# Talking-heads attention into routed experts: 512-column products in the experts' first layer, and another order at the loop's end

## Chip, cores and metric

One core of a Trainium2 chip runs the whole program. The metric is the device time of one execution in microseconds (us), and the median of several runs is compared. Its engines are TensorE (PE in the profile, with PEld for its weight loads), VectorE (DVE), ScalarE (ACT), GpSimd (POOL) and SyncE (SP). SP issues the plain DMAs, and POOL issues the indirect ones (gathers and scatters by index).

## What is computed

Attention first, with 4 batches, 12 heads, 448 positions and 64 values a head. Heads are mixed before and after the softmax. The result is then laid out as 1792 tokens of 768 values, and each token goes through one of 8 experts:

```python
scores = np.einsum('bhij,hg->bgij', scale * q @ k.T, w_pre)
attn = softmax(scores)
attn = np.einsum('bhij,hg->bgij', attn, w_post)
x = (attn @ v).transpose(0, 2, 1, 3).reshape(1792, 768)

logits = normed(x) @ normed(expert_emb).T / tau
expert_idx = np.argmax(logits, axis=1)
gate_w = softmax(logits)[token, expert_idx]
for e in range(8):
    mask = expert_idx == e
    h = np.maximum(x[mask] @ w1[e], 0.0)              # 768 -> 1024
    out[mask] = gate_w[mask, None] * (h @ w2[e])      # 1024 -> 768
```

## The kernel before, in words

**Attention.** The tokens are cut into 16 tiles of 120 or 90 positions, and a tile into 5 or 6 steps, 92 steps in all. A step of the loop multiplies q by k (L262), mixes heads (L297), takes the softmax (L305, L314), mixes again and transposes (L340, L345) and evicts the result `a` to SBUF (L358 on ACT, L360 on DVE). One tile later the product with v follows (`emit_av`, L376). Its sum lies in one PSUM bank (`ps_a`, one buffer), which `emit_xT_evict` (L388, on ACT) copies out. `emit_xlog` (L394) transposes it back and makes the routing logits, and `emit_x` (L406) and `store_x` (L414) write tokens to `x_tok` in DRAM.

**The order** of everything is written out by hand: each engine runs its instructions in the order in which the program lists them, and waits inside its queue for what it needs. Side work of the loop is held in generators that are advanced twice a step: `route_early` (positions of the first 10 tiles within their experts; its last product is `p_i`, L538), `gate_value` (gates; eight small stores into `g_tok`, L494), `first_x` (gather of the first expert's first rows, L604, and of their gates, L610, on POOL), `mid`. A bank for them is taken only at steps that `pes_at` leaves free.

**Weights.** All expert products are float32r products of split numbers: a weight is split into `wh` and the rest `wl`, x into `xh` and `xl`, h into `hh` and `hl`. `w_split` does one slice of 128 weight rows: `wh` on ACT (L590), `wl` on DVE (L591). It also issues the DMA (L575, on SP) of slices up to four ahead, into four `raw_w` buffers, each of which comes free when its `wl` is done. An expert has 14 slices: 8 of w2 (768 columns, 384 KB) and 6 of the next expert's w1 (1024 columns, 512 KB).

**Experts.** Expert 0 and the last, overflow tile (128 rows whose expert is chosen at run time) go through `ffn_tok`. It keeps rows of x on the weight side and multiplies 512 columns of w1 at a time (L644); then `relu`, a transpose `tr` (L653, evicted as `hh` on ACT, L656, and `hl` on DVE, L657) and products with w2 (L663). Calls to `w_split` stand between its steps. Experts 1 to 7 have 256 rows each: `emit_g1` keeps w1 on the weight side. For each of 8 blocks of 128 columns and each of 6 slices it makes three products of 256 columns (wh by xh, wh by xl, wl by xh, L1049) into half a bank. A pair of blocks fills a bank, which is evicted by `hh` (ACT, L1051) and `hl` (DVE, L1052). After each pair `during_g1` transposes part of the next expert's x (`fill`: L624, L629, L630), does two splits and one step of `route_late` (positions of overflow rows; pairs of L1138, L1139 on DVE). `emit_g2` multiplies by w2 (L1067) for two halves `j` of the rows and two halves `n0` of the columns, scales by the gate (L1069) and scatters (L697).

Of the kernel before, what the change touches and what calls it, by code (L numbers as in the profile page):

```python
# [32 lines left out]
MAXO = 12  # L33
# [14 lines left out]
def talking_heads_moe(  # L48
# [81 lines left out]
    with tc.manual_schedule():  # L130
# [409 lines left out]
        def route_early(bank, wait):  # L540
# [9 lines left out]
            pairs = yield from place(re, p, 0, NE)  # L550
            yield from wait()
# [62 lines left out]
        def emit_xT(pool, xgs):  # L614

            b = 1 if pool is xa_p else 2
            xh = pool.tile([128, KD, 128 * b], FR, tag="xh", name="xh", bufs=b)[:, :, :128 * len(xgs)]
            xl = pool.tile([128, KD, 128 * b], FR, tag="xl", name="xl", bufs=b)[:, :, :128 * len(xgs)]
# [15 lines left out]
            return (xh, xl), [lambda j=j, k0=k0: step(j, k0) for j in range(len(xgs)) for k0 in (0, 3)]  # L634
# [148 lines left out]
        for t in range(NTL - 1):  # L783
# [5 lines left out]
            for k, p in ((0, b0 + 2), (1, b0 + ln - 1)):  # L789
                if k and t == NTL - 2:  # L790
                    continue
                acts.setdefault(p, []).append(lambda t=t, k=k: emit_xT_evict(t, k))
# [127 lines left out]
        emit_xT_evict(LT - 1, 1)  # L920
# [8 lines left out]
        w_split(V, 2)  # L929
        w_split(V, 2)  # L930
        for a in range(3):
            emit_av(LT, a)
        late_lo = []
        w_split(V, 2, late_lo.append)
        w_split(V, 2, late_lo.append)
        run(gens[-1][0])
        for f in late_lo:
            f()
        emit_xlog(LT - 1, 1)
        emit_xT_evict(LT, 0)  # L940
        emit_lgc(LT - 1, 1)
        emit_x(LT - 1, 1)
        store_x(LT - 1)
# [55 lines left out]
        for f in late_lo:  # L999
            f()  # L1000
# [3 lines left out]
        xT, fill = emit_xT(mp, xg[0])  # L1004
        slots(iv, 0, 2 * E)
# [30 lines left out]

        def emit_g1(xT, w, after):
            xh, xl = xT
# [3 lines left out]
            for f0 in range(0, KF, 2):  # L1042
                p = ps_h.tile([128, 512], F32, tag="p", name="p_h").rearrange("p (f n) -> p f n", n=n)
                for f in range(2):
                    c = slice((f0 + f) * 128, (f0 + f + 1) * 128)
                    for k in range(KD):
                        wh_, wl_ = w[k]
                        for i, (lt, rt_) in enumerate(((wh_, xh), (wh_, xl), (wl_, xh))):
                            T.matmul(p[:, f], lt[:, c], rt_[:, k], start=(k == 0 and i == 0), stop=(k == KD - 1 and i == 2))  # L1049
                o = (slice(None), slice(f0, f0 + 2))  # L1050
                A.activation(out=hh[o], in_=p, func=ACTF.Relu)  # L1051
# [21 lines left out]
        def route_late():  # L1073
# [55 lines left out]
            for t in range(NTL + 2):  # L1129
                if t > 1:  # L1130
                    T.matmul(xb[:, 16:16 + MAXO], *hot[t - 2], start=(t == 2), stop=(t == NTL + 1))
# [131 lines left out]
```

## Time and profile before

| | |
|---|---|
| three runs | 716.62, 713.16 and 710.42 us (median 713.16) |
| profiled execution | 712.93 us, its span 711.1 us |
| mean granted TensorE clock | 0.987 of full speed |
| PE busy | 676.7 us, 95% of the span |
| DVE busy | 463.2 us, 65% |
| ACT busy | 393.6 us, 55% |
| POOL busy | 119.1 us, 17% |
| DMA | 134.61 MB, 189 GB/s on average |

The span runs from the first to the last instruction; the execution's own time has 1.83 us more around it. Busy shares are averages over the attention loop (to about 378 us), the end of the loop and expert 0 (378 to 430 us), experts 1 to 7 (430 to 677 us), the overflow tile (677 to 700 us) and a tail with the last scatter.

### The profile page before, as it was taken

How to read it: one execution, taken by the hardware profiler on the slowest of the kernel's cores; microseconds unless marked ns; L12 is line 12 of the kernel's file. 1: busy time of each engine (PE TensorE's matmuls, PEld its weight loads, DVE VectorE, ACT ScalarE, POOL GpSimd, SP SyncE). 2: the span in 40 equal slices, each digit the busy share in tenths (PEclk: the TensorE clock that was granted, in tenths of full speed). 3: DMA queues.
4: the chain of work that ended last, by engine and by line, in shares of the span. 5: the costliest groups of instructions: out<-in, count | busy, mean ns of one | idle time of the engine just before them, and what ended most of it. 6: DMA issues, size and time to landing. Idle time of an engine off the chain costs nothing. (4 is left out here: it accounts for less than half of the span.)

```text
span 711.1 us, 25384 instructions
## 1 busy us (share of the span) xinstructions
PE 676.7 (95%) x10796; PEld 559.6 (79%) x10796; DVE 463.2 (65%) x1076; ACT 393.6 (55%) x775; POOL 119.1 (17%) x179
## 2 busy tenths in 40 slices
PE   9799999999999999989998899999999999999983
PEld 4366776776777777767777789999999999999973
DVE  6477666666667666886676765868665656474651
ACT  2466676667767676756676453635262636353540
POOL 7021010110111011101201213430203030100000
PEclk9899999999999999999999999999999999999997
DMA  7687567655667556643614755867676767575750
GB/s 224 187 247 214 150 197 212 194 171 160 194 201 212 177 162 193 202 134 116 214 47 128 261 164 154 292 206 224 205 227 213 233 216 233 182 235 170 249 155 15
DMA packets 60361, 134.61 MB, mean 189 GB/s; under 512 B 7067, under 2 KB 38411, under 8 KB 60246
## 3 DMA queue, kind: packets, MB, share of 16 engines
q1 hardware_dynamic: 56126, 119.56, 54.7%
q0 software_dynamic: 3520, 12.44, 5.2%
q8 instruction: 86, 1.41, 0.8%
q10 hardware_dynamic: 600, 0.97, 0.4%
q14 instruction: 29, 0.24, 0.1%
HBM read 83.21 MB, written 12.20 MB: 134 GB/s over the span
## 5 line engine op out<-in xcount | busy, mean ns | idle before, releaser
L305 DVE TENSOR_REDUCE mn<-p_p 128x1 f32<-128x448 f32 (+1 forms) x182 | 105.6, 619 | 91.2 <-PE p_p L297 90.4
L590 ACT ACTIVATE wh<-raw_w 128x768 fp32r<-128x768 f32 (+2 forms) x132 | 114.9, 904 | 45.5 <-DMA raw_w<-w 42.6
L591 DVE TENSOR_TENSOR wl<-raw_w,wh 128x768 fp32r<-128x768 f32 (+2 forms) x132 | 131.0, 1026 | 9.4 <-ACT wh L590 9.1
L270 ACT ACTIVATE s<-p_q 128x896 f32<-128x896 f32 (+1 forms) x89 | 80.8, 909 | 91.3 <-PE p_q L262 81.4
L314 ACT ACTIVATE e<-p_p,mn 128x448 f32<-128x448 f32 (+1 forms) x182 | 113.5, 628 | 31.9 <-DVE mn L305 28.0
L340 PEld LDWEIGHTS p_m<-wr,e 64*64 64x64 f32 x4320 | 84.0, 135 | 44.8 <-issue 41.7
L360 DVE COPY a<-p_m 128x420 f32<-128x420 f32 (+1 forms) x182 | 95.0, 562 | 2.8 <-PE p_m L345 2.6
L1049 PE MATMUL p_h<-xh,wh 128*128 128x256 f32 x336 | 96.8, 288 | 0.0
L262 PE MATMUL p_q<-k,q 64*64 64x448 f32 x768 | 96.4, 569 | 0.3 <-ACT s L270 0.3
L376 PE MATMUL p_av<-a,v 128*64 128x120 f32 (+3 forms) x1920 | 92.0, 248 | 3.1 <-issue 2.0
L1049 PE MATMUL p_h<-xh,wl 128*128 128x256 f32 x336 | 94.9, 283 | 0.0
L1049 PE MATMUL p_h<-xl,wh 128*128 128x256 f32 x336 | 94.7, 282 | 0.0
L297 PE MATMUL p_p<-g,wpre_sb 64*64 64x448 f32 (+1 forms) x712 | 89.4, 544 | 5.1 <-DMA g<-s 4.7
L376 PEld LDWEIGHTS p_av<-a,v 128*64 128x64 f32 x1920 | 83.3, 137 | 9.3 <-issue 3.8
L340 PE MATMUL p_m<-wr,e 64*64 64x60 f32 x4320 | 85.1, 219 | 3.7 <-issue 1.7
L325 POOL TENSOR_TENSOR wr<-wpost_sb,r 128x120 f32<-128x120 f32 (+1 forms) x92 | 35.5, 386 | 314.1 <-DVE r L324 218.2
L1067 PE MATMUL p_o<-wh,hh 128*128 128x384 f32 x224 | 75.8, 338 | 0.0
L1067 PE MATMUL p_o<-wh,hl 128*128 128x384 f32 x224 | 75.0, 335 | 0.0
L1067 PE MATMUL p_o<-wl,hh 128*128 128x384 f32 x224 | 75.0, 335 | 0.0
L1051 ACT ACTIVATE hh<-p_h 128x512 fp32r<-128x512 f32 x28 | 16.7, 598 | 100.6 <-PE p_h L1049 63.6
L297 PEld LDWEIGHTS p_p<-g,wpre_sb 64*64 64x64 f32 (+1 forms) x712 | 30.2, 134 | 43.2 <-issue 31.4
L1049 PEld LDWEIGHTS p_h<-xl,wh 128*128 128x128 f32 x336 | 63.6, 189 | 0.0
(209 smaller groups left out, 951.1 us busy)
## 6 DMA issues: line engine op xcount, KB each, us to landing
g<-s SPq DMA_DIRECT2D x144, 210.0 KB
raw_w<-w SPq DMA_DIRECT2D x54, 512.0 KB
raw_w<-w SPq DMA_DIRECT2D x72, 384.0 KB
v<-vP SPq DMA_DIRECT2D x24, 320.0 KB
g<-s SPq DMA_DIRECT2D x42, 157.5 KB
k<-kT SPq DMA_DIRECT2D x24, 224.0 KB
q<-qT SPq DMA_DIRECT2D x26, 192.0 KB
x_tok<-xs SPq DMA_DIRECT2D x22, 180.0 KB
```

The lines of the kernel that those rows point to most:

```text
L262: T.matmul(p[r][64 * w:64 * w + 64, :S], q_sb[t][64 * r:64 * r + 64, a, w, :], k_sb[t // 4, a][64 * r:64 * r + 64], start=True, stop=True)
L270: A.activation(out=o, in_=i, func=ACTF.Copy)
L297: T.matmul(p[w][64 * x:64 * x + 64, :S], wpre_sb[64 * w:64 * w + 64 - 4 * w], g[64 * w:64 * w + 64 - 4 * w, m + x if nx == 2 else m], star ...
L305: V.tensor_reduce(out=mn[q, c:c + 1], in_=p[u][q, :S], op=ALU.max, axis=AX.X, negate=True)
L314: A.activation(out=e[q, c], in_=p[u][q, :S], func=ACTF.Exp, bias=mn[q, c:c + 1], accum_out=sums[q, c:c + 1])
L340: T.matmul(pm[x][q[c], u * 240 + jt * 60:u * 240 + jt * 60 + 60], e[q[x], u, jt * 128 + 64 * c:jt * 128 + 64 * c + 64], wr[q[x], u], start ...
L360: V.tensor_copy(out=o, in_=i)
L376: T.matmul(p[64 * r:64 * r + 64, u], v_sb[t // 4, a][:, jt, r * D:(r + 1) * D], at[:, jt * 12 + c::48][:, :2] if jt < 3 else at[:, 36 + c] ...
L590: A.activation(out=h[:, c], in_=r[:, c], func=ACTF.Copy)
L591: lo = lambda: eng.tensor_tensor(out=l[:, c], in0=r[:, c], in1=h[:, c].bitcast(F32), op=ALU.subtract)
L1049: T.matmul(p[:, f], lt[:, c], rt_[:, k], start=(k == 0 and i == 0), stop=(k == KD - 1 and i == 2))
L1067: T.matmul(p[:, :384], lt[:, k, c], rt_[:, m], start=(k == 0 and i == 0), stop=(k == KF - 1 and i == 2))
```

## The change

- `route_early` pauses twice more between `place` and its last product.
- `emit_xT` puts xh and xl of a slice side by side in one tile `xx`.
- At the loop's end the second half of tile 14 is evicted (L388) inside the last step, ahead of that step's weight split on ACT. Its `emit_xlog` goes ahead of the products of tile 15 with v, and its `emit_x`, logits and store directly behind the first three of these. Two half splits move back by some places.
- In expert 0 one step of `ffn_tok` (its first `tr` among others) goes ahead of two `wl` operations and two small operations on DVE.
- In `emit_g1` each slice is two products: wh by xh and xl together, 512 columns wide, and wl by xh, 256 columns, added onto the half that holds wh by xl. Each block of 128 columns has a bank of its own, in turn two of `ps_h` and the one of `ps_a`. To evict it, ACT copies the second half out (`hx`) and DVE adds the first (`hs`); `hh` and `hl` are then made from the pair of sums in SBUF.
- In `emit_g2` the first half of the rows runs six slices for both column halves and then the last two for both.
- Splits: seven during `emit_g1`, seven during `emit_g2`. `route_late` is advanced in `emit_g1` from expert 2 on only, and its products follow their DVE operations by four tiles where it was two.
- In the overflow tile three splits that stood ahead of the first `tr` go behind it.

```diff
             pairs = yield from place(re, p, 0, NE)
+            yield
+            yield
             yield from wait()
             p = bank("p_i")
...
             for k, p in ((0, b0 + 2), (1, b0 + ln - 1)):
+                acts.setdefault(p, []).append(lambda t=t, k=k: emit_xT_evict(t, k))
                 if k and t == NTL - 2:
                     continue
-                acts.setdefault(p, []).append(lambda t=t, k=k: emit_xT_evict(t, k))
...
         evict()
-        emit_xT_evict(LT - 1, 1)
...
         closing.append(True)
-        w_split(V, 2)
+        emit_xlog(LT - 1, 1)
         w_split(V, 2)
         for a in range(3):
             emit_av(LT, a)
+        emit_x(LT - 1, 1)
+        emit_lgc(LT - 1, 1)
+        store_x(LT - 1)
         late_lo = []
         w_split(V, 2, late_lo.append)
         w_split(V, 2, late_lo.append)
         run(gens[-1][0])
+        emit_xT_evict(LT, 0)
         for f in late_lo:
             f()
-        emit_xlog(LT - 1, 1)
-        emit_xT_evict(LT, 0)
-        emit_lgc(LT - 1, 1)
-        emit_x(LT - 1, 1)
-        store_x(LT - 1)
+        w_split(V, 2)
         w_split(V, 2)
         emit_sq(LT - 1, rt)
...
-        for f in late_lo:
-            f()
         w1p[1] = weight(w1, 1, KD, F, "a")
...
         xT, fill = emit_xT(mp, xg[0])
+        steps_of(st_a, 1)
+        for f in late_lo:
+            f()
         slots(iv, 0, 2 * E)
...
             for f0 in range(0, KF, 2):
-                p = ps_h.tile([128, 512], F32, tag="p", name="p_h").rearrange("p (f n) -> p f n", n=n)
+                hs = mp.tile([128, 2, n], F32, tag="hs", name="hs", bufs=1)
                 for f in range(2):
+                    p = ps_a.tile([128, 512], F32, tag="a", name="p_h") if turn[0] % 3 == 2 else (
+                        ps_h.tile([128, 512], F32, tag="p", name="p_h"))
+                    turn[0] += 1
                     c = slice((f0 + f) * 128, (f0 + f + 1) * 128)
                     for k in range(KD):
-                        wh_, wl_ = w[k]
-                        for i, (lt, rt_) in enumerate(((wh_, xh), (wh_, xl), (wl_, xh))):
-                            T.matmul(p[:, f], lt[:, c], rt_[:, k], start=(k == 0 and i == 0), stop=(k == KD - 1 and i == 2))
+                        wide = (p, w[k][0][:, c], xx[:, k].rearrange("p a n -> p (a n)"))
+                        small = (p[:, n:], w[k][1][:, c], xh[:, k])
+                        for i, m in enumerate((wide, small) if k < KD - 1 else (small, wide)):
+                            T.matmul(*m, start=(k == 0 and i == 0), stop=(k == KD - 1 and i == 1))
+                    hx = mp.tile([128, n], F32, tag="hx", name="hx", bufs=2)
+                    A.activation(out=hx, in_=p[:, n:], func=ACTF.Copy)
+                    V.tensor_tensor(out=hs[:, f], in0=p[:, :n], in1=hx, op=ALU.add)
                 o = (slice(None), slice(f0, f0 + 2))
-                A.activation(out=hh[o], in_=p, func=ACTF.Relu)
-                V.scalar_tensor_tensor(out=hl[o], in0=p, scalar=0.0, in1=hh[o].bitcast(F32), op0=ALU.max, op1=ALU.subtract)
+                A.activation(out=hh[o], in_=hs, func=ACTF.Relu)
+                V.scalar_tensor_tensor(out=hl[o], in0=hs, scalar=0.0, in1=hh[o].bitcast(F32), op0=ALU.max, op1=ALU.subtract)
                 after(f0 // 2)
...
-                for n0 in range(2):
-                    p = ps_m.tile([128, 512], F32, tag="m", name="p_o")
+                p = {}
+                for n0, ks in ((0, range(6)), (1, range(6)), (0, range(6, KF)), (1, range(6, KF))) if j == 0 else (
+                        (0, range(KF)), (1, range(KF))):
...
+                    if ks[-1] == KF - 1:
+                        V.tensor_scalar(out=o[:, m], in0=p[n0], scalar1=gj[:, 0:1], scalar2=None, op0=ALU.mult)
+                        after(2 * j + n0)
+                    else:
+                        w_split(V)
...
             def during_g1(q):
...
                 w_split(V)
-                w_split(V)
-                next(late, None)
+                if q < 3:
+                    w_split(V)
+                if e > 1:
+                    next(late, None)
...
             def during_g2(q):
                 if q < 3:
                     w_split(V)
+                if q < 2:
                     w_split(V)
                 next(late, None)
...
         for i, _ in enumerate(ffn_tok(xT, w1p[E], w2p[E], gg[E][0], idx_s[:, 2 * E:2 * E + 1])):
-            if i != KD - 1:
-                w_split(V)
-            if i == KD:
+            if i < KD - 1 or i in (2 * KD - 2, 2 * KD, 2 * KD + 1):
                 w_split(V)
```

## Rows read from the trace of the kernel before

**Rows 1.** Busy time by stretch: us, each engine (instructions), PEclk, DMA share, GB/s.

```profile
398.00:410.00 12.00, 10.08 (x60) 9.43 (x59) 7.49 (x12) 4.52 (x8) 4.09 (x3) 1.00 0.94 343
430.00:686.00 256.00, 256.00 (x1816) 253.62 (x1816) 163.92 (x254) 117.04 (x159) 51.55 (x43) 1.00 0.69 221
686.00:692.00 6.00, 3.27 (x11) 2.58 (x10) 3.47 (x4) 2.78 (x5) 0.00 (x0) 0.77 0.05 22
```

**Rows 2.** Waits of PE, 290 to 400 us: waiter, releaser, total, times, longest.

```profile
PE p_i L538 <- DVE ohs L532: 0.9, 1, 0.9
```

**Rows 3.** Timeline of PE, first layer of expert 1: start, duration; twelve products apart.

```profile
439.87 0.28 PE L1049 MATMUL p_h<-xh,wh 128*128 128x256 f32 x1
...
441.31 0.28 PE L1049 MATMUL p_h<-xh,wh 128*128 128x256 f32 x1
```

**Rows 4.** Timeline of PE, first layer of expert 0: again twelve products apart.

```profile
389.37 0.40 PE L644 MATMUL p_h<-wl,xh 128*128 128x512 f32 x1
...
392.11 0.39 PE L644 MATMUL p_h<-wl,xh 128*128 128x512 f32 x1
```

**Rows 5.** Timeline of DVE, first layer of expert 3.

```profile
511.58 0.69 DVE L1052 SCALAR_TENSOR_TENSOR hl<-p_h,hh 128x512 fp32r<-128x512 f32 x1 [1.04 <-ACT hh L1051]
512.19 0.55 DVE L630 TENSOR_TENSOR xl<-p_t,xh 128x384 fp32r<-128x384 f32 x1
512.69 1.83 DVE L591 TENSOR_TENSOR wl<-raw_w,wh 128x768 fp32r<-128x768 f32 x2
516.33 0.69 DVE L1052 SCALAR_TENSOR_TENSOR hl<-p_h,hh 128x512 fp32r<-128x512 f32 x1 [1.81 <-ACT hh L1051]
```

**Rows 6.** Timeline of ACT, the same stretch.

```profile
510.95 0.60 ACT L1051 ACTIVATE hh<-p_h 128x512 fp32r<-128x512 f32 x1 [2.33 <-PE p_h L1049]
511.44 0.49 ACT L629 ACTIVATE xh<-p_t 128x384 fp32r<-128x384 f32 x1
```

**Rows 7.** Groups of ACT, 425 to 700 us: count, busy us, mean ns, idle before.

```profile
L590 ACT ACTIVATE wh<-raw_w 128x768 fp32r<-128x768 f32 x64 | 51.0, 846 | 7.2 <-DMA raw_w<-w 6.1 <-SPq L1186 1.0
L590 ACT ACTIVATE wh<-raw_w 128x1024 fp32r<-128x1024 f32 x45 | 47.8, 1062 | 34.2 <-DMA raw_w<-w 32.5 <-DVE ohp L1138 0.8 <-DVE wl L591 0.4
```

**Rows 8.** Groups of DVE, 425 to 700 us: one operation of a late-routing pair.

```profile
L1139 DVE TENSOR_SCALAR ohs<-io,mo,tv 128x12 f16<-128x12 f32 x16 | 4.6, 290 | 0.0
```

**Rows 9.** Timeline of PE at the end of the loop.

```profile
378.00 0.30 PE L345 MATMUL p_m<-wr,e 64*64 64x60 f32 x4
379.46 2.30 PE L376 MATMUL p_av<-a,v 128*64 128x90 f32 x60 [1.16 <-ACT xT L388]
...
382.15 0.94 PE L394 MATMUL p_x<-ien,xT 128*120 128x136 f32 x6
...
386.51 0.93 PE L394 MATMUL p_x<-ien,xT_l 128*90 128x136 f32 x6 [0.30 <-ACT xs L406]
```

**Rows 10.** Timeline of ACT and of DVE at the last step.

```profile
376.37 0.61 ACT L590 ACTIVATE wh<-raw_w 128x512 fp32r<-128x512 f32 x1
...
376.97 1.29 DVE L591 TENSOR_TENSOR wl<-raw_w,wh 128x512 fp32r<-128x512 f32 x2
```

**Rows 11.** Timelines of PE and ACT in expert 0, first tile.

```profile
399.72 0.45 PE L663 MATMUL p_o<-wh,hl 128*128 128x384 f32 x1 [1.48 <-DVE hl L657]
...
402.57 0.85 ACT L590 ACTIVATE wh<-raw_w 128x768 fp32r<-128x768 f32 x1 [1.81 <-DMA raw_w<-w]
```

**Rows 12.** Timelines of SP and POOL: the gates' stores, and their first gather.

```profile
335.43 3.33 SPq L494 DMA_DIRECT2D g_tok<-gt__6303  x8
...
353.52 1.01 POOL L610 DMA_INDIRECT gg<-g_tok,idx_a  x1 [0.30 <-issue]
```

**Rows 13.** Timelines of DVE and PE in the overflow tile.

```profile
686.16 2.91 DVE L591 TENSOR_TENSOR wl<-raw_w,wh 128x768 fp32r<-128x768 f32 x3 [1.20 <-ACT wh L590]
688.62 0.44 PE L663 MATMUL p_o<-wh,hh 128*128 128x384 f32 x1 [2.06 <-ACT hh L656]
689.73 0.69 PE L663 MATMUL p_o<-wh,hl 128*128 128x384 f32 x1 [0.67 <-DVE hl L657]
```

More of the change, by code (lines that the diff above doesn't have):

```diff
@@ L616, in emit_xT @@
             b = 1 if pool is xa_p else 2
-            xh = pool.tile([128, KD, 128 * b], FR, tag="xh", name="xh", bufs=b)[:, :, :128 * len(xgs)]
-            xl = pool.tile([128, KD, 128 * b], FR, tag="xl", name="xl", bufs=b)[:, :, :128 * len(xgs)]
+            xx = pool.tile([128, KD, 2, 128 * b], FR, tag="xx", name="xx", bufs=b)
+            xh, xl = (xx[:, :, i, :128 * len(xgs)] for i in range(2))
             def step(j, k0):
@@ L633, in step @@
                 split()
-            return (xh, xl), [lambda j=j, k0=k0: step(j, k0) for j in range(len(xgs)) for k0 in (0, 3)]
+            return (xh, xl, xx), [lambda j=j, k0=k0: step(j, k0) for j in range(len(xgs)) for k0 in (0, 3)]
         def ffn_tok(xT, w1, w2, gg, ix, held=None):
@@ L1035, in talking_heads_moe @@
         rows_of(2, x=False)
+        turn = [0]
         def emit_g1(xT, w, after):
-            xh, xl = xT
+            xh, _, xx = xT
             n = xh.shape[2]
@@ L1060, in emit_g2 @@
                 c = slice(128 * j, 128 * j + 128)
[L1061 to L1062 removed]
+                p = {}
+                for n0, ks in ((0, range(6)), (1, range(6)), (0, range(6, KF)), (1, range(6, KF))) if j == 0 else (
+                        (0, range(KF)), (1, range(KF))):
                     m = slice(384 * n0, 384 * n0 + 384)
[L1064 removed]
+                    if ks[0] == 0:
+                        p[n0] = ps_m.tile([128, 512], F32, tag="m", name="p_o")[:, :384]
+                    for k in ks:
                         wh_, wl_ = w[k]
                         for i, (lt, rt_) in enumerate(((hh, wh_), (hl, wh_), (hh, wl_))):
[L1067 removed]
+                            T.matmul(p[n0], lt[:, k, c], rt_[:, m], start=(k == 0 and i == 0),
                                      stop=(k == KF - 1 and i == 2))
[L1069 to L1070 removed]
+                    if ks[-1] == KF - 1:
[3 more added lines that the diff above has]
+                        w_split(V)
                 scatter(ix, o)
@@ L1128, in route_late @@
             hot = []
-            for t in range(NTL + 2):
-                if t > 1:
-                    T.matmul(xb[:, 16:16 + MAXO], *hot[t - 2], start=(t == 2), stop=(t == NTL + 1))
-                if t == NTL:
-                    yield
+            for t in range(NTL + 4):
+                if t > 3:
+                    T.matmul(xb[:, 16:16 + MAXO], *hot[t - 4], start=(t == 4), stop=(t == NTL + 3))
                 if t >= NTL:
+                    if t % 2:
+                        yield
                     continue
-                ohp = rt.tile([128, 128], F16, tag="ohp", name="ohp", bufs=4)
-                ohs = rt.tile([128, MAXO], F16, tag="ohs", name="ohs", bufs=4)
+                ohp = mp.tile([128, 128], F16, tag="ohp", name="ohp", bufs=6)
+                ohs = mp.tile([128, MAXO], F16, tag="ohs", name="ohs", bufs=6)
                 V.tensor_scalar(out=ohp, in0=io128, scalar1=po[:, t:t + 1], scalar2=None, op0=ALU.is_equal)
```

4 lines of the change are left out of this document (removed).

## The prediction

> **What bounds the kernel now.** I first read busy time by stretch, since the kernel has stages with different limits. In experts 1 to 7 PE is busy all of 256.00 us with the full clock granted, while DVE is busy 163.92 us and ACT 117.04 us [rows 1]. So there only PE's own pace counts, and what the other engines do matters only if PE comes to wait for it. A busy PE can still hide its pace, because its products overlap. I therefore read start times: twelve 256-column products take 441.31 - 439.87 = 1.44 us, 120 ns each [rows 3], although one lasts 280 ns. Twelve 512-column products take 392.11 - 389.37 = 2.74 us, 228 ns each [rows 4]. The granted clock is 1.00 [rows 1], the upper level of 2.4 GHz, at which the columns alone are 107 and 213 ns; some 13 to 15 ns come with each product. For 384 columns, halfway, I take 174 ns.
>
> Outside that stretch PE does wait. The list of waits and the timelines name the places: 0.9 us at `p_i` in the loop [rows 2], 1.16 us at the loop's end [rows 9], 1.48 us in expert 0 [rows 11], and two waits in the overflow tile, after which the clock falls [rows 1, 13]. The stretch of 398 to 410 us is different: DMA is busy 0.94 of the time at 343 GB/s [rows 1], so there PE also follows the weights.
>
> **Part by part**, each against the profiled execution of 712.93 us, which is 0.23 us under the median of the three runs.
>
> *Early routing.* PE stands 0.9 us before `p_i` until `ohs` is done [rows 2]. With two more pauses `p_i` is emitted behind further work. By the steps that `pes_at` leaves free it goes from step 75 to 78, and the gates behind it from 78 to 81; its ten products stay. Gain 0.9 us, between 0 and 0.9. The gates' eight stores move with it, on SP, from behind the placements of one step to behind those of a later one and ahead of the first weight loads. A step is at most 378 / 92 = 4.1 us, so they are issued by 335.43 + 12.3 = 347.7 and are through 3.33 us later, at 351.1 us. Their first reader is a gather at 353.52 us [rows 12]. That leaves 2.4 us for landing; I cost the move at nothing, and price the end of that cover below.
>
> *The loop's end.* The eviction of tile 14 now stands on ACT ahead of the last step's weight split. It must wait for products that stand just ahead of the last step's own (of which the last start at 378.00 [rows 9]), so by my estimate the split (0.61 us, at 376.37 before) runs at about 378.2 to 378.8. Behind it on DVE wait its `wl`, which was the second of the two at 376.97, and the copies of `a` behind that [rows 10]. So tile 15's first product with v starts at about 380.0 where it was 379.46 [rows 9]: 0.55 us lost. Against it, the six `p_x` products (382.15, about 0.87 us to the next start [rows 9]) move into that idle time, and the next use of their bank at 386.51 no longer waits for a late `xs` (0.30 us idle by the row, some 0.5 us by start times [rows 9]). Together 0.87 + 0.5 - 0.55 = 0.8, call it 0.9 us with a smaller wait behind it. The store of tile 14's tokens is issued sooner on SP, ahead of some weight loads; it is short, and I cost it at nothing (a load that it holds up would wait for ACT's copy, under 1 us). Bounds: 0, if the copies come later still; 1.5, if they aren't delayed.
>
> *Expert 0, first tile.* PE stands 1.48 us until `hl` is done [rows 11], which is queued on DVE behind two `wl`. The change moves it ahead of them, so this wait goes, and a smaller one at the second `hl`. But the two `wl` then end some 1 us later, and with them two `raw_w` buffers come free. The slices that are loaded into these are already late: `wh` waits 1.81 us for one [rows 11], in the stretch where DMA is nearly full. What is late next is thus the w2 slices 6 and 7, and the gather of the next rows. I keep 0.6 us, between 0 (all goes to the DMA) and 2.1.
>
> *Experts 1 to 7.* There are 7 x 8 x 6 = 336 slices. Three products of 256 columns cost 3 x 120 = 360 ns, the new pair 228 + 120 = 348 ns: 336 x 12 ns = 4.0 us. The columns stay the same, only one product's fixed part goes. The Trainium skill ("TensorE: Matmul & The Clock Gate", section "Back-to-back issue gap") speaks against even that: it gives columns over 2.4 GHz plus about 2.5 ns, by which the saving would be an estimated 0.8 us and the sum 706.0 us. The trace differs, with 120 and 228 ns [rows 3, 4].
>
> The price is the eviction. No row shows an addition of 256 columns; `xl`, 384 columns with an operand in PSUM too, holds DVE 0.50 us and `hl`, 512 columns, 0.61 us [rows 5], so I take 0.40. The copy `hx` I take as 0.38, from 0.49 and 0.60 us [rows 6]. DVE's round for a pair is then two additions 0.8, a wait for the relu 0.7, `hl` 0.61, `xl` 0.50, two splits 1.83: 4.45 us. PE's round is 516.33 - 511.58 = 4.75 us now [rows 5] and 4.6 after. So DVE just keeps up. Where late routing adds its four small operations (about 0.2 us apart, at most 0.29 [rows 8]) the round is 5.3 us, and DVE falls behind 0.7 us a pair; that is expert 3, and half as much expert 2. Two things absorb it. With three banks a block may be evicted two blocks (4.2 us) late. And `emit_g2` now needs the last two slices of h only after 2 x 6 x 3 x 0.174 = 6.3 us, while the chain behind the last block takes about 2.1 us. In expert 3 the lag could still hold back the scaling that frees a bank for the second half of the rows, so I take off 0.5 us: 3.5 us, between 2 and 4.0. The redistributed splits keep 14 an expert; the last w1 split stands where one of the last two stood, so it ends no later.
>
> *Overflow tile.* Its first `hh` on ACT and `hl` on DVE stand behind three splits: three `wl` fill DVE from 686.16 [rows 13]. PE's last product before it starts at about 686.16, so it could go on at 686.4; it goes on at 688.62, 2.2 us. The next is at 689.73, 1.11 us later instead of 0.17, 0.9 us. Then the granted clock is 0.77 over 686 to 692 [rows 1], which is 2.8 us at the lower level, 1.2 GHz; from 689.73 to 692 that costs half of 2.27, 1.1 us. With the splits behind the first `tr`, both evictions run while PE does its last first-layer products, no idle stretch is left such as the clock fell after, and the three slices are needed 4 us later. Gain 2.2 + 0.9 + 1.1 = 4.2, between 3.3 (a small wait left, clock down all the same) and 4.4. What follows PE's end is untouched.
>
> Sum: 0.9 + 0.9 + 0.6 + 3.5 + 4.2 = 10.1 us, 712.93 - 10.1 = **702.8 us**.
>
> **Rivals.**
> *A. The new eviction becomes the bound; slower than before.* Place: ACT and DVE in `emit_g1`. `hx` and the relu stand on ACT behind the `wh` of the pair before, so a `wh` that waits for its slice now holds back banks. If w2's slices came late as w1's do (32.5 us over 45, 0.7 each [rows 7]), a round were 4.45 + 1.4 = 5.9 us. With a slack of about 4.1 us over four pairs, PE loses time from a round of 4.6 + 4.1 / 4 = 5.6 us on, and at 6.4 us, which longer additions would add, 7 x (4 x 1.8 - 4.1) = 22 us: 725 us. Against it: w2's slices wait only 6.1 us over 64 [rows 7], and ACT idles 2.33 us before `hh` [rows 6].
> *B. The wide product saves nothing.* If the part beyond the columns belongs to the columns or to the mixing of widths, the 4.0 us fall away: 706.8 us. For it stands only that no row has the two widths in turn; against it that 120 and 228 ns differ by no more than the columns.
> *C. A wait is handed on in the loop.* The gather of gates stands on POOL ahead of `wr`, on which the next step's products wait. If the stores land after 353.5 us, up to the 3.3 us of their issue come back [rows 12]: 706.1 us.
>
> **How the numbers follow.** The forecast has 0.73, A 0.07, B 0.08, C 0.12. All upper bounds together give 12.9 us, 700.0; all lower ones 5.3 us, 707.6. With the scatter of a median the range is 699 to 708 us, which takes in B and C. About 1% (7.1 us) is what a measurement of this kernel tells from no change. Below 706 lie nine tenths of the forecast and half of B and C: faster 0.76. Slower is A's upper part, 0.06; the rest, 0.18, is within 1%.
>
> **What the profile after would show.** Starts of wide and narrow products 348 ns apart a pair, and PE without idle time from the first `emit_g1` to the overflow tile; DVE idle little in `emit_g1` of expert 3. `p_i` without a wait before it. `p_x` of tile 14 in the gap before tile 15's products. In the overflow tile, `p_o` directly behind `p_h` and the clock at its upper level. I would be wrong if PE waits in `emit_g1` for a bank (A), if the pair takes 360 ns (B), if `wr` waits behind the gathers near 353 us (C), or if expert 1's first product, at 430.0 us now, comes less than 1.5 us earlier (0.9 + 0.9 + 0.6 = 2.4 are forecast).

## The result and the profile after

Twelve executions each gave a median of 709.61 us (700.12 to 714.20) after the change and 714.17 us (709.59 to 719.63) before it. The ratio is 0.9891, with an interval of 0.9856 to 0.9926: faster by 1.1%, some 7.8 us. It leaves out executions that lie more than 1.5% above the fastest of their kernel, which are five of the twelve after the change and none of the twelve before, so by the medians of all of them the gain is smaller, 4.6 us. Taken from the profiled 712.93 us, the 7.8 us give 705.2 us, where 702.8 was forecast. The profiled execution of the changed kernel took 703.52 us (span 701.7, mean granted clock 0.986), 9.4 us less than the one before.

By stretch, for [rows 1] (the first layers and the tiles now stand a few us earlier):

```profile
397.00:409.00 12.00, 11.44 (x66) 10.24 (x65) 8.10 (x13) 5.38 (x9) 4.17 (x4) 1.00 0.93 322
427.50:683.50 256.00, 256.00 (x1493) 237.14 (x1493) 186.82 (x313) 139.59 (x219) 50.29 (x43) 1.00 0.68 221
681.00:687.00 6.00, 6.00 (x36) 5.70 (x35) 4.03 (x5) 3.23 (x5) 0.00 (x0) 1.00 0.02 8
```

Over the experts' 256 us PE is still busy throughout, while DVE has gone from 163.92 to 186.82 us and ACT from 117.04 to 139.59. The last stretch shows the overflow tile: PE busy all of 6.00 us at clock 1.00, where it was 3.27 us at 0.77.

Timeline of PE in the loop and at its end, for [rows 2, 9]:

```profile
330.06 0.41 PE L538 MATMUL p_i<-ohs,ohp 128*128 128x16 f16 x10
...
378.07 0.27 PE L340 MATMUL p_m<-wr,e 64*64 64x60 f32 x2 [0.93 <-issue]
...
378.44 0.96 PE L394 MATMUL p_x<-ien,xT 128*120 128x136 f32 x6
379.33 2.30 PE L376 MATMUL p_av<-a,v 128*64 128x90 f32 x60
...
385.14 0.86 PE L394 MATMUL p_x<-ien,xT_l 128*90 128x136 f32 x6
```

`p_i` starts with no wait ahead of it. `p_x` of tile 14 stands in the gap, and tile 15's products follow it at 379.33 without the wait of 1.16 us. What was not forecast is the 0.93 us just ahead, in which PE waits inside the last step for nothing that the profile names.

Timeline of PE at the start of expert 1, for [rows 3]:

```profile
427.51 0.40 PE L1057 MATMUL p_h<-xx,wh 128*128 128x512 f32 x1
427.74 0.28 PE L1057 MATMUL p_h<-xx,wl 128*128 128x256 f32 x1
...
428.91 0.39 PE L1057 MATMUL p_h<-xx,wh 128*128 128x512 f32 x1
```

From the first to the fifth wide product of a block lie four pairs: 1.40 us, 350 ns a pair. The wide one holds the place for 233 ns (the median from start to start over experts 1 to 7), not 228. Expert 1 begins at 427.51 us, 2.5 us earlier (2.4 was forecast).

Timeline of DVE in expert 3, for [rows 5], one round of a pair of blocks with late routing in it:

```profile
508.78 0.69 DVE L1063 SCALAR_TENSOR_TENSOR hl<-hs,hh 128x512 fp32r<-128x512 f32 x1 [0.70 <-ACT hh L1062]
509.39 0.55 DVE L632 TENSOR_TENSOR xx<-p_t,xx 128x384 fp32r<-128x384 f32 x1
509.89 1.83 DVE L593 TENSOR_TENSOR wl<-raw_w,wh 128x768 fp32r<-128x768 f32 x2
...
512.42 0.75 DVE L1060 TENSOR_TENSOR hs<-p_h,hx 128x256 f32<-128x256 f32 x2
513.87 0.69 DVE L1063 SCALAR_TENSOR_TENSOR hl<-hs,hh 128x512 fp32r<-128x512 f32 x1 [0.70 <-ACT hh L1062]
```

Two additions take 0.75 us (0.8 was forecast), and the round 513.87 - 508.78 = 5.09 us (5.3).

Timeline of PE in the overflow tile, for [rows 13]:

```profile
681.20 0.40 PE L646 MATMUL p_h<-wl,xx 128*128 128x512 f32 x1
681.43 0.34 PE L665 MATMUL p_o<-wh,hh 128*128 128x384 f32 x1
681.61 0.45 PE L665 MATMUL p_o<-wh,hl 128*128 128x384 f32 x1
```

`p_o` starts 0.23 us behind the last `p_h`, where 2.46 us lay between them.

**The same stages in every profile.** From start times in the traces, in us: *loop*, from the eight `p_p` that start at 312.21 us before (312.34 after) to expert 0's first product with w2; *tile 1*, from there to the next tile's first product; *tile 2*, to expert 1's first; *experts*, to the overflow tile's first product; *overflow*, from there to its last scaling.

```
                  loop   tile 1  tile 2  experts  overflow
before           85.68   11.93   20.17   247.52   22.47
after            84.08   10.93   20.16   245.00   18.03
e1_changed       83.85   12.99   20.18   245.50   19.41
e2_narrow        83.94   14.16   20.17   247.54   17.94
e3_tail_old      83.87   13.88   20.14   244.94   23.18
e4_wide_only     84.31   11.45   20.18   252.76   22.36
e5_lo_old        83.81   11.88   20.15   245.49   19.50
e6_gath          85.37   11.07   24.73   245.52   18.22
e7_grouped       83.82   14.73   20.17   245.61   17.94
e8_add2          83.80   11.44   20.15   269.98   20.55
e9_mid           85.11   12.32   20.18   245.41   18.36
e10_mid_early    84.97   14.48   20.15   245.70   18.15
e11_mid_next     85.59   11.15   19.22   245.31   18.06
e12_three        85.45   11.52   19.19   245.03   17.93
```

Between the two profiled executions the stages give 1.6 + 1.0 + 0.0 + 2.5 + 4.4 = 9.5 us. The other rows show which of these are the change's and which are one execution's luck. What lies ahead of 312 us is not touched by the change; there the profiles scatter too, and reach that place between 309.4 and 319.9 us.

### The profile page after: what moved, and what is told of

The parts are those of the page before. It is cut to its first block, busy times and chain, and to the rows that moved or that the text cites. A ratio compares the mean times of both kernels' runs of the same rounds, so it can differ in the third digit from the quotient of the medians.

```text
span 701.7 us, 24824 instructions
## 1 busy us (share of the span) xinstructions
PE 674.6 (96%) x10460; PEld 541.8 (77%) x10460; DVE 483.8 (69%) x1132; ACT 414.2 (59%) x831; POOL 118.0 (17%) x179
## 5 line engine op out<-in xcount | busy, mean ns | idle before, releaser
L1057 PE MATMUL p_h<-xx,wh 128*128 128x512 f32 x336 | 120.2, 400 | 0.0
L1057 PE MATMUL p_h<-xx,wl 128*128 128x256 f32 x336 | 85.1, 280 | 0.0
L1057 PEld LDWEIGHTS p_h<-xx,wh 128*128 128x128 f32 x336 | 61.1, 188 | 10.3
L1057 PEld LDWEIGHTS p_h<-xx,wl 128*128 128x128 f32 x336 | 63.3, 188 | 3.8
L699 POOL DMA_INDIRECT out<-o,idx_s x17 | 23.1, 1359 | 211.0 <-DVE o L1084 159.2
```

The costliest lines, as they stand in the source:

```text
L1057: T.matmul(*m, start=(k == 0 and i == 0), stop=(k == KD - 1 and i == 1))
```

## The experiments

The labels are those of the table. Ratios are against the kernel before, run on the same chip.

**e1_changed**: the changed kernel itself. 

> The changed kernel once more, as the mark for the others on this chip. Theory 1 (PE's waits at four places and a small saving in the first layer add up): a span 8 to 10 us under that of before, of which 4.4 us fall in the overflow tile, 2.5 us in experts 1 to 7, 1.0 us in expert 0's first tile and 1.5 us in the loop and at its end. Rival 2 (the profiled pair flatters it, and one of these stages was only a good execution): the stages come out otherwise in this second profile, and the ratio of times is nearer to 0.995 than to 0.988.

Median 709.98 us, ratio 0.9881 (0.9828 to 0.9935): the gain repeats. Its profile differs from the first one in two stages above all: tile 1 takes 12.99 us for 10.93, overflow 19.41 for 18.03 (and experts 245.50 for 245.00). Its five stages add up to 5.8 us less than those before the change, where the first profile gave 9.5. Waits of PE in tile 1:

```profile
PE p_o L665 <- ACT wh L592: 1.5, 2, 1.3
PE p_o L665 <- DVE wl L593: 0.8, 2, 0.4
```

So PE follows the weights there, and in the overflow tile `ht` stands on ACT behind a `wh` whose slice came late (timelines of ACT and PE; SPq L1204 is SP at the end of the program, which waits for the same slice):

```profile
682.23 0.84 ACT L592 ACTIVATE wh<-raw_w 128x768 fp32r<-128x768 f32 x1 [2.72 <-SPq L1204]
682.98 0.58 ACT L650 ACTIVATE ht<-p_h 128x512 f32<-128x512 f32 x1
...
683.61 0.65 PE L655 MATMUL p_t<-id_sb,ht 128*128 128x128 f32 x4 [1.26 <-ACT ht L650]
```

**e2_narrow**: three narrow products a slice, the new eviction kept.

```diff
-                        for i, m in enumerate((wide, small) if k < KD - 1 else (small, wide)):
-                            T.matmul(*m, start=(k == 0 and i == 0), stop=(k == KD - 1 and i == 1))
...
+                    one = [(p[:, :n], w[k][0][:, c], xx[:, k, 0]) for k in range(KD)]
+                    two = [(p[:, n:], w[k][i][:, c], xx[:, k, 1 - i]) for k in range(KD) for i in range(2)]
+                    for ms in (one, two):
+                        for i, m in enumerate(ms):
+                            T.matmul(*m, start=(i == 0), stop=(i == len(ms) - 1))
```

> The changed kernel with its whole eviction, banks and splits, but each slice again as three products of 256 columns (first the six of wh by xh, then the twelve into the other half). Theory 1: PE sets the pace and a wide product in turn with a narrow one takes 233 + 118 ns against 3 x 119.5, so each g1 stage is 48 x 8 ns = 0.4 us longer and the whole 2.7 us longer than the changed kernel. The price as predicted (12 ns) would give 4.0 us. Rival (the eviction sets the pace of the first layer by now): no difference.

Median 711.41 us, ratio 0.9970 (0.9932 to 1.0009). *Experts* take 247.54 us, as before the change (247.52), and PE waits for nothing in them. So the new eviction costs PE nothing, and the wide products alone give 247.54 - 245.00 = 2.5 us, 7.6 ns for each of 336 slices; against e1_changed, where PE waits a little in expert 1, it is 2.0 us.

**e3_tail_old**: the overflow tile's splits in their old places.

```diff
-            if i < KD - 1 or i in (2 * KD - 2, 2 * KD, 2 * KD + 1):
+            if i != KD - 1:
+                w_split(V)
+            if i == KD:
                 w_split(V)
```

> The changed kernel with the overflow tile's splits where they stood before, three of them ahead of the first transpose. Theory 1: 4.4 us longer than the changed kernel, all of it between the overflow tile's first and last product, with the clock at its lower level again for some 3 us. Rival (the gap closes by itself, since the last w1 splits end sooner in the changed order): under 1 us.

Median 712.17 us, ratio 0.9938 (0.9891 to 0.9984). *Overflow* takes 23.18 us, 0.7 more than before the change, since here too a slice came late; against the changed kernel's 18.03 and 19.41 that is 5.2 and 3.8 us. So the gain in this stage comes from the place of the splits.

**e4_wide_only**: the kernel before with the new `emit_g1` and `emit_xT` alone; `emit_g2`, the places of the splits and late routing are the old ones.

> The kernel before with the 512-column products and their eviction alone: all eight w2 splits in emit_g1, emit_g2 slice by slice, late routing from expert 1 on, everything else old. Theory 1: without the new order in emit_g2 the last two h slices and the last w2 slice are needed 3 to 4 us after the last first-layer product and are ready after 3 to 5 us, so PE waits some 0.5 to 1 us an expert; the saving of 2.7 us is used up: within 2 us of before, and 1 to 4 us slower than it in experts 1 to 7 where late routing runs too. Rival (the covers are not needed): 2.7 us faster than before with no wait of PE in experts 1 to 7.

Median 718.28 us, ratio 1.0072 (1.0030 to 1.0114): slower. *Experts* take 252.76 us, 5.2 more than before the change. Waits of PE there:

```profile
PE xb L1140 <- DVE ohs L1148: 1.3, 4, 0.7
PE p_o L1076 <- ACT xx L629: 1.1, 1, 1.1
PE p_o L1076 <- DVE wl L591: 0.4, 1, 0.4
```

These are late routing's products, two tiles behind their DVE operations, and `emit_g2`'s. Where the list names no wait, an expert without late routing still takes 17.14 us from its first to its last product with w2, for 16.56 to 16.58, and the steps that grow are those of slices 6 and 7 in its first quarter. So the eviction alone would have cost more than the wide products give; the changed order in `emit_g2` and in late routing pays for it.

**e5_lo_old**: in expert 0 the two `wl` and two small operations stand ahead of the first `hl` again.

```diff
+        for f in late_lo:
+            f()
         w1p[1] = weight(w1, 1, KD, F, "a")
...
-        steps_of(st_a, 1)
-        for f in late_lo:
-            f()
         slots(iv, 0, 2 * E)
```

> The changed kernel with one part undone: in expert 0 the two wl operations and the small operations on DVE stand ahead of the first hl again, as before the change. The part of the program from expert 0's first product with w2 to the next tile's first product took 11.93 us before and 11.45 us in the run with wide products alone (old order), but 10.93, 12.99, 14.16 and 13.88 us in the four profiles of the new order, where PE waits up to 1.3 us for a wh whose slice came late. Theory 1 (buffers): the new order ends two wl later, their raw_w buffers come free later, and slices 6 and 7 land later; so here that part takes about 11.5 us with a wait of 1.5 us for hl and none for a late wh, expert 1 begins 1 to 2.5 us earlier by the profile than in most runs of the changed kernel, and the median is 0 to 2 us lower than the changed kernel's. Theory 2 (gathers): the two gathers of the next expert's rows, which now start about 2 us earlier, take the DMAs from slices 6 and 7; then the wh stays late here too, the wait for hl comes on top, and this part takes 13 us or more. Theory 3 (chance): the times of this part scatter by 3 us whatever the order; then it lies anywhere in 11 to 14 us.

Median 708.27 us, ratio 0.9910 (0.9875 to 0.9945). *Tile 1* takes 11.88 us: the wait for `hl` is back, and no `wh` comes late. Its list of waits of PE in tile 1 has one line:

```profile
PE p_o L665 <- DVE hl L659: 1.9, 2, 1.3
```

The three profiles with the old order lie at 11.45 to 11.93 us (e12_three, below, at 11.52); the six with the changed order and the gathers as they were at 10.93, 11.44, 12.99, 13.88, 14.16 and 14.73 us.

**e6_gath**: the gathers of expert 1's rows wait on POOL for the `wh` of slice 6.

```diff
-        rows_of(1, g=False)
...
+        tie = mp.tile([128, 1], F32, name="tie", bufs=1)
+        G_.tensor_copy(out=tie, in_=w2p[0][6][0][:, :1].bitcast(F32))
+        rows_of(1, g=False)
```

> The changed kernel, but the two gathers of expert 1's rows (768 KB together) wait on POOL for the wh of slice 6 of w2 of expert 0, which PE waits for in most profiles of the changed kernel. Theory 1 (buffers): slices 6 and 7 are late because their loads start late; they land as late as before, and the part from the first product with w2 to the next tile stays at 13 us, or grows, if the next rows now come late (the next tile begins with their transposes). Theory 2 (gathers): the loads of slices 6 and 7 have the DMAs to themselves, 384 KB of gathers at 300 to 340 GB/s each take about 1.2 us, so the wh come 1 to 2.4 us sooner and the part takes 10.5 to 11.5 us.

Median 710.78 us, ratio 0.9995 (0.9958 to 1.0031). *Tile 1* takes 11.07 us, and slice 7 is there directly behind slice 6 (timeline of ACT; in e1_changed their `wh` were 2.7 us apart, at 402.16 and 404.90):

```profile
401.46 1.82 ACT L592 ACTIVATE wh<-raw_w 128x768 fp32r<-128x768 f32 x2 [2.01 <-DMA raw_w<-w]
```

But slice 6 comes 401.46 - 395.96 = 5.5 us behind the first product with w2 as in the changed kernel (5.4 and 5.7 in its two profiles), not 4.7 as before the change. The price is *tile 2*: its rows are late, and the clock falls behind that wait (timeline of PE; busy time of that stretch):

```profile
411.03 0.87 PE L626 MATMUL p_t<-id_sb,xg 128*128 128x128 f32 x3 [3.15 <-DMA xg<-x_tok,idx_g]
...
407.00:421.70 14.70, 11.55 (x54) 9.31 (x53) 4.78 (x18) 3.65 (x7) 3.06 (x3) 0.88 0.46 158
```

So slice 6 is late without these gathers too; what is left of the change is its load, issued 1.10 us behind that product where it was 0.08 us ahead of it before. For slice 7 this one profile decides nothing. In the changed kernel's first profile, in e7_grouped and in e8_add2 its `wh` also starts 0.95 to 0.99 us behind slice 6's, with the gathers where they were.

**e7_grouped**: per block five wide products, the six narrow ones, the last wide one.

> The changed kernel with another order of the same products in a block of the first layer: five wide ones, the six narrow ones, the last wide one; nothing else. In the changed kernel a wide product takes about 233 ns by start times where it follows a narrow one, and the pair 351 ns, where 228 + 120 = 348 was forecast. Theory 1 (what follows what sets it): a wide product behind a wide one takes 228 ns, so four of six gain 5 ns, a block 0.02 us, 56 blocks 1.1 us: experts 1 to 7 take 243.9 us for 245.0. Theory 2 (it is the length, and what stands before plays no part): no change, 245.0 us. Theory 3 (the weight load of 128 columns behind a narrow product doesn't fit): six narrow ones in a row take over 120 ns each, and the stretch grows.

One execution, 712.49 us. *Experts* take 245.61 us, no less. Timeline of PE, one block:

```profile
577.92 1.33 PE L1058 MATMUL p_h<-xx,wh 128*128 128x512 f32 x5
579.09 0.88 PE L1058 MATMUL p_h<-xx,wl 128*128 128x256 f32 x6
579.81 0.40 PE L1058 MATMUL p_h<-xx,wh 128*128 128x512 f32 x1
```

Five wide ones in a row take 579.09 - 577.92 = 1.17 us, 234 ns each, and six narrow ones 120 ns each. So what stands ahead of a product makes no difference that shows.

**e8_add2**: two more additions of 256 columns on DVE a block, their results unused.

```diff
+                    for _ in range(2):
+                        hj = mp.tile([128, n], F32, tag="hj", name="hj", bufs=1)
+                        V.tensor_tensor(out=hj, in0=p[:, :n], in1=hx, op=ALU.add)
                     V.tensor_tensor(out=hs[:, f], in0=p[:, :n], in1=hx, op=ALU.add)
```

> The changed kernel with two more additions of 256 columns on DVE per block, whose results are not used: 4 x 0.37 = 1.5 us more per pair of blocks. DVE's round of a pair then is about 5.9 us (4.4 + 1.5), in expert 3 with late routing 6.6 us, against PE's 4.54 us. Theory 1 (with three banks and the new order of the second layer DVE may lag some 4.1 us over an expert): an expert's first layer then loses 4 x (5.9 - 4.54) - 4.1 = 1.3 us, expert 3's 4.1 us, about 12 us in all, and experts 1 to 7 take about 257 us for 245. Theory 2 (no slack, each pair waits): 28 x 1.4 = 38 us and more, 283 us. Theory 3 (DVE's lag is hidden, since it has the second layer to catch up): 245 to 248 us.

One execution, 734.40 us. *Experts* take 269.98 us, 25.0 more. Two rounds of DVE behind one another are 601.25 - 595.37 = 5.88 us apart by the starts of `hl`, and an expert without late routing takes 37.64 us for 34.89. PE's own round is 18.13 / 4 = 4.53 us (first layer of expert 1 to its first product with w2), so four rounds are 4 x (5.88 - 4.53) = 5.4 us too long and 2.75 us are lost: some 2.6 us an expert were absorbed. The slack is real, and smaller than the 4.1 us that were forecast. PE's waits there, the largest first, are those of rival A:

```profile
PE p_h L1057 <- DVE hs L1063: 10.0, 9, 2.0
PE p_o L1084 <- DVE wl L593: 3.4, 7, 0.9
```

**e9_mid**: one of the two `wl` ahead of the first `hl`, the other behind it.

```diff
+late_lo.pop(0)()
 w1p[1] = weight(w1, 1, KD, F, "a")
```

> The changed kernel with half of expert 0's edit undone: one wl stands ahead of the first hl on DVE, the other and the small operations behind it. With both behind it, slice 6 of w2 is at its wh 5.4 to 5.7 us after the first product with w2 (402.16 - 396.51 in the second profile of the changed kernel), with both ahead 4.7 us before the change and 4.6 in the run with the order undone; DVE stands 0.67 us idle before that hl. Theory 1 (buffers): the first wl fits into that idle time, its raw_w buffer comes free about 1.4 us earlier, so wh of slice 6 comes near 4.6 us, hl only some 0.2 us later than in the changed kernel, and the part from the first product with w2 to the next tile takes 10.3 to 11.3 us, where it took 10.93 to 14.73 us in the changed order and 11.5 to 11.9 us in the old one. Theory 2 (the gathers alone hold up the slices): wh of slices 6 and 7 as late as in the changed kernel, 11 to 14 us.

Median 710.40 us, ratio 0.9889 (0.9842 to 0.9935). *Tile 1* takes 12.32 us, and 11.15 in e11_mid_next, which has this order too. The load that was held up is issued 0.28 us ahead of the first product with w2 (400.59 for 400.87 us), as in the old order (397.81 for 397.89), where the changed kernel issues it 1.10 us behind (397.52 for 396.42). Yet the `wh` of slice 6 starts 5.6 us behind that product. So slice 6 is late without a late load too; what still differs from the old order is the gathers, of which the last two start at 401.88 and 403.20 us here, 1.0 and 2.3 us behind that product, and 2.0 and 3.8 us behind it before the change (399.87, 401.70). With e6_gath this fits that either of the two is enough by itself to hold up slice 6; no run shows it directly.

**e10_mid_early**: the same, with the first of the four splits that follow one step earlier.

```diff
-        for _ in range(4):
-            steps_of(st_a, 2)
+        for i in range(4):
+            steps_of(st_a, 2 if i else 1)
             w_split(V)
```

> As the one before, and the first of the four splits that follow stands one step of expert 0 earlier, where it stood before the change: in the changed kernel the wh of slice 4 starts 0.70 us after the first product with w2 (397.21 - 396.51), behind the relu of the second half, and before the change 0.71 us ahead of it (397.18 - 397.89). Theory 1: its wl comes sooner too, so w1's slices for the next expert are loaded sooner, and the small waits for wl at slices 6 and 7 (0.4 to 0.5 us each) shrink: 0 to 0.5 us less than the run before. Theory 2: the split that now stands ahead of the relu delays the second hh and hl by its 0.85 us, and PE waits for these: 0 to 0.9 us more.

Median 710.73 us, ratio 0.9958 (0.9924 to 0.9993). Theory 2, and by more than its 0.9 us: *tile 1* takes 14.48 us, 2.2 more than in e9_mid, and the list has what that order hands on, a second `hh` behind a `wh` that waits for its slice:

```profile
PE p_o L665 <- ACT hh L658: 2.1, 1, 2.1
```

**e11_mid_next**: e9_mid with one split of expert 0's second tile left to a later place (`if i >= 11 and i % 2 and i != 15`).

> As the first of these three, and one split in expert 0's second tile, whose wl stands ahead of the second hl, is left to a later place. PE waits 0.94 us there in every profile, before and after the change (1.11 us from the product with hh to that with hl, where 0.17 would do). Theory 1: the wait is DVE's queue, and goes: 0.9 us less up to expert 1's first product, and the later split finds its time in expert 1. Theory 2: the slice that comes later is then missed in expert 1, and PE waits for it in its first layer: nothing gained.

Median 708.19 us, ratio 0.9922 (0.9883 to 0.9960). *Tile 2* takes 19.22 us for 20.18 and *experts* 245.31: the 0.94 us are gained and don't come back. In the changed kernel that wait stood here (timeline of PE):

```profile
422.30 0.42 PE L665 MATMUL p_o<-wh,hh 128*128 128x384 f32 x1
423.40 0.45 PE L665 MATMUL p_o<-wh,hl 128*128 128x384 f32 x1 [0.69 <-DVE hl L659]
```

**e12_three**: e5_lo_old, the later split of e11_mid_next, and in the overflow tile one split moved from ahead of `ht` to behind the first `hh` (`if i < KD - 2 or 2 * KD - 2 <= i < 2 * KD + 2`).

> The changed kernel with three edits that the runs so far point to: expert 0's first hl stands behind the two wl again (that run took 11.88 us from the first product with w2 to the next tile, without a late wh); one split of expert 0's second tile comes later (the 0.94 us wait for the second hl was gone, 9.0 us where that half took 9.8, and nothing came back in expert 1); and in the overflow tile the last of the five splits ahead of the first relu ht moves behind the first hh (in the runs with a late slice of w2 ht stands on ACT behind a wh that waits up to 2.9 us, and PE loses 1.3 to 1.4 us before the first tr). Theory 1 (each is a wait of its own): first tile 11.5 to 11.9 us, second tile 19.0 to 19.3 us where it was 20.0 to 20.2, from the overflow tile's first product to its last scaling 18.0 us whether or not the slice is late; against the changed kernel's usual execution 1 to 3 us less, a median of 707 to 709 us where the changed kernel's were 709.6 and 710.0. Theory 2 (the waits are handed on, since that stretch follows the DMAs): the first tile or expert 1 gives the 0.9 us back, and the second relu of the overflow tile now waits behind that wh; the median is 709.5 to 711 us.

Median 705.17 us (700.93 to 707.91, six executions), ratio 0.9849 (0.9807 to 0.9891): 1.5% faster than the kernel before, with the lowest median of all. Against the changed kernel the medians are 4.4 and 4.8 us lower, though the intervals of the ratios overlap, so that it beats the changed kernel is likely and not shown. *Tile 1* 11.52, *tile 2* 19.19, *overflow* 17.93 us, as theory 1 had it. Timeline of ACT in the overflow tile:

```profile
679.15 0.85 ACT L592 ACTIVATE wh<-raw_w 128x768 fp32r<-128x768 f32 x1 [0.96 <-DMA raw_w<-w]
680.24 0.60 ACT L650 ACTIVATE ht<-p_h 128x512 f32<-128x512 f32 x1 [0.25 <-PE p_h L646]
683.49 0.60 ACT L658 ACTIVATE hh<-p_t 128x512 fp32r<-128x512 f32 x1 [2.65 <-PE p_t L655]
683.99 1.57 ACT L592 ACTIVATE wh<-raw_w 128x768 fp32r<-128x768 f32 x2
```

`ht` now waits for PE alone.

## Why the prediction was right, and where it was not

The sign held, and at their own places four of the five terms did in the main. The whole came out at 7.8 us by the ratio and 4.6 by the medians instead of 10.1, because one term had the wrong sign in most executions, one was 1.0 to 1.5 us too large, and the loop lost part of its gain at a place that the forecast had put at nothing. That the two profiled executions lie 9.4 us apart, close to the forecast, is luck: the stages of e1_changed give 5.8 us.

*Early routing, 0.9 us.* The wait of 0.9 us is gone in every profile with the new order; e4_wide_only, which has the old one, shows it at 0.8. Net, from the `p_p` at 312.21 us before to those at 349.87, it is 37.66 us before, 36.97 in e4_wide_only, whose order there is the same, and 36.47 in the changed kernel: 0.5 to 1.2 us, about what was forecast. Rival C did not happen: the eight stores of gates are issued at 345.54 us and through in 3.32 us (347.7 and 351.1 were the latest forecast), and POOL goes on to `wr` directly behind the gather.

*Loop's end, 0.9 us.* From the loop's last `p_p` to expert 0's first product with w2 it is 27.87 us before, 27.89 in e4_wide_only, and 26.94 to 26.97 in e1_changed, e2_narrow and e3_tail_old: 0.9 us. The profiled execution after has 27.47, for its 0.93 us without a named cause (e11_mid_next has 0.78 us there). The copies that were to come late do: those profiles show a wait of 0.6 us of `p_av` behind ACT's `wh`, which the forecast put at 0.55.

*The loop as a whole.* The two gains at their places do not add up in the stage. It takes 85.68 us before the change, but 84.31 in e4_wide_only, which has neither of the two edits; the changed order takes 83.80 to 84.08 us in seven profiles and 84.97 to 85.59 in five. Of the 1.4 us between the two profiles with the old order, 0.7 lie ahead of the `p_p` at 349.87 us; most of the rest is an idle time a few us behind it (last section), 0.72 us before the change and none in e4_wide_only. In every profile with the new order it is 0.78 to 2.29 us. The forecast put the move of the gates' stores at nothing. On SP they now stand directly ahead of the first four weight loads, which are issued at 348.97 us where it was 346.63, and DMA is full in the step with the idle time, where it was half free (kernel before, then the changed one; busy time of that step):

```profile
353.03:358.69 5.66, 4.38 (x109) 3.18 (x105) 2.83 (x8) 2.88 (x7) 1.98 (x4) 1.00 0.48 178
351.98:357.69 5.71, 4.37 (x109) 3.19 (x105) 2.83 (x8) 2.90 (x7) 1.99 (x4) 1.00 0.96 365
```

Whether the later loads lengthen the idle time was not tried: no run undoes one of the two edits at the loop by itself.

*Expert 0, first tile, 0.6 us, between 0 and 2.1.* This is the step that failed. "All goes to the DMA" was taken as the worst case, 0. In the profiles of the changed kernel's order the tile gained 1.0 us once, 0.5 in e8_add2, and lost 1.1 to 2.8 in the four others. The step named what would be late, slices 6 and 7 and the gathers, but not that an order which brings the gathers forward and the loads back, in a stretch where DMA is busy 0.87 to 0.97 of the time, can make the slices later than they were. In three of those four the clock then goes down behind the wait; over the tile e2_narrow has 0.88 granted.

```profile
403.80:417.96 14.16, 12.32 (x59) 10.71 (x58) 8.15 (x13) 5.34 (x8) 3.42 (x3) 0.88 0.87 309
```

That the order is the cause shows in slice 6: its `wh` starts 4.1 to 4.7 us behind the first product with w2 in all four profiles with the old order (before, e4_wide_only, e5_lo_old, e12_three), and 5.4 to 7.6 us behind it in all seven with the changed one. Which part of the order does it, the later loads or the earlier gathers, stays open: slice 6 is as late with the gathers out of the way (e6_gath) as with its load issued in time (e9_mid).

*Experts 1 to 7, 3.5 us.* They gave 2.5, and 2.0 in e1_changed. The mechanism was right, the term was mis-sized: over a whole first layer with its transposes it is 18.13 us against 18.49 in e2_narrow, so that a slice saves 7.5 ns and not 12. The wide product was priced too low. The 228 ns of [rows 4] come from the fastest stretch of expert 0; the overflow tile of the same kernel has 234 ns (last section), and 360 - 234 - 118 = 8 ns a slice would have made the term 2.7 us, with 118 ns for the narrow product as measured after the change. The 0.5 us taken off for DVE's lag in expert 3 were not lost (e2_narrow). Rival B is so far true that a wide product costs 5 to 6 ns more than was taken, but not by the mixing of widths (e7_grouped). By the 2.5 ns a product that the Trainium skill ("TensorE: Matmul & The Clock Gate", section "Back-to-back issue gap") gives, the saving was an estimated 0.8 us; the runs lie between that and the forecast. Rival A did not happen, and its point was nearer than forecast: a round of about 4.53 + 2.6 / 4 = 5.2 us, not 5.6, and expert 3 stands at 5.09.

*Overflow tile, 4.2 us.* It gave 4.4 between the profiled pair, and 3.1 in e1_changed, where a late slice holds `ht`. The gain is then below the bound of 3.3, because the split ahead of `ht` was left out of the account.

## What to carry to other kernels

Where a stretch follows the DMAs, moving an operation ahead in one engine's queue also moves buffers, loads and gathers: ask of each transfer when it is issued relative to its reader, and let the term go below zero. Ahead of an eviction that PE waits for, keep no work that itself waits for a load (`wh` ahead of `ht`, `wl` ahead of `hl`): there the wait comes in some executions only, and one profile may not show it. An eviction that is made longer needs its cover in the same edit, as e4_wide_only shows. And price a product from more than one stretch of the trace.

## What the runs showed of the hardware

A 512-column float32r product behind another one takes about 225 to 240 ns from start to start at a granted clock of 1.00. It is 234 ns in `emit_g1`, behind a narrow or a wide one. In `ffn_tok`, where the roles of weights and x are exchanged, it is 228 ns in the stretch of expert 0 that [rows 4] shows, but 234 ns in the overflow tile: twelve of them take 683.83 - 681.02 = 2.81 us there. So the roles are not the reason; what makes the one stretch faster is open. Timeline of PE, kernel before:

```profile
681.02 0.40 PE L644 MATMUL p_h<-wh,xh 128*128 128x512 f32 x1
...
683.83 0.39 PE L644 MATMUL p_h<-wh,xh 128*128 128x512 f32 x1
```

In the loop PE stands for a while at the same place, between the first and the second product with v of one step (it goes on at 353 to 364 us), for nothing that the profile names, and for very unequal times: 0.72 us before the change, 0.78 to 2.29 us in the profiles with the changed order, and not at all in e4_wide_only. Timelines of PE in e5_lo_old and in e6_gath, whose code there is the changed kernel's, and the granted clock over the step that follows:

```profile
354.36 1.91 PE L376 MATMUL p_av<-a,v 128*64 128x120 f32 x39 [2.10 <-issue]
356.20:359.14 2.94, 2.94 (x76) 2.26 (x74) 1.92 (x4) 1.68 (x5) 0.00 (x0) 1.00 0.03 9
```

```profile
354.55 2.48 PE L376 MATMUL p_av<-a,v 128*64 128x120 f32 x39 [2.29 <-issue]
356.97:360.92 3.95, 3.95 (x74) 2.72 (x73) 2.15 (x4) 1.90 (x6) 0.00 (x0) 0.73 0.02 6
```

In all thirteen traces with this idle time, one 16 KB transfer of the DMA queue that the profile calls instruction ends 1.2 to 1.6 us ahead of the product that goes on (355.26 for 356.85 us before, 353.17 for 354.55 in e6_gath). So PE seems to wait for its instructions; this was not tried.

The idle time by itself does not make the 1.2 to 1.8 us by which *loop* differs between kernels that are the same up to there. It is as long in e5_lo_old, e7_grouped and e8_add2 (2.09 to 2.12 us, *loop* 83.80 to 83.82) as in e6_gath and the four runs from e9_mid on (2.01 to 2.29 us, *loop* 84.97 to 85.59). What differs is the clock: in these five it falls to its lower level behind the idle time, to a mean of 0.91 and 0.73 over two steps in e6_gath, and in the other three it stays at 1.00. Why it falls in some and not in others after the same idle time is not shown.
